# High parts of the first operands written by GpSimd's DMA queue, cast on the way

## The chip, the cores and the metric

One core of one Trainium2 chip runs the whole kernel. The metric is the device time of that core in microseconds. Before the change the median of three runs was 393.45 us (393.07 to 393.51); one further execution was taken with the profiler, and its own time was 392.84 us. All positions in time below count from the start of the profiled span.

## What is computed

Two branches work on the same tokens x (2048 x 448), and a gate mixes them:

```
g   = sigmoid((x * gate_w).sum(-1))                 # one number per token
qkv = x @ wqkv                                      # 448 -> 3 x 448, 16 heads of 28
a   = softmax(q . k over 8 earlier tokens, step 2) . v, then @ wo
b   = relu(x @ w1 + b1)^2 @ w2 + b2                 # 448 -> 1792 -> 448
out = g * a + (1 - g) * b
```

Everything is float32.

## The kernel before

**Splitting.** TensorE multiplies in the type float32r, which keeps fewer bits than float32. So each operand is held as a high part (the float32 value copied into a float32r tile) and a low part (raw value minus high part, again float32r), and each product is made of three matmuls: high times high, high times low, low times high. ACT usually makes the high part by a Copy, DVE the low part by a `tensor_sub`. The raw float32 data must be in SBUF for both.

**Order of the work.** The tokens are cut into four chunks of 512. The inner dimension of 448 is cut in three tiles of 128 (k = 0, 1, 2) and a rest of 64 (written `x7`, `x8` for the tokens' high and low part, `w7h`, `w7l` for the weights). Chunk 0's q projection is the first real work (`qkv_first`, lines 415 to 443): for each k it does, for tokens 0-1 and then 2-3 of the four token tiles (for k > 0 all four at once), `x.h` times `wqh`, `x.h` times `wql`, `x.l` times `wqh`. That is 12 matmuls for each k, 36 in all, all issued at line 429. Each has 452 columns. After them come the rest of 64 rows and then all other projections, as pairs of half-height matmuls from line 341. The order of TensorE's instructions is the order of the program.

**The start.** Line 806 issues `WARM` = 19 matmuls on zeros (256 columns each), which have nothing to wait for. Beside them the first data come in. ACT's queue brings the first k tile of chunk 0's tokens in two halves (`rx[:, 0]`, line 813; 128 partitions x 256 numbers, 128 KB each). SP's queue brings, one after the other, the first weights for k = 0 (`raws[0][:, 0]`, line 816, 225 KB), weights k = 1, tokens k = 1 (line 821, 256 KB), weights k = 2, tokens k = 2, the weights' rest in two pieces (line 819), the tokens' rest, and then six tiles of further weights (line 825) and one more (line 828). GpSimd's queue brings nothing.

Lines 830 to 843 then make high and low parts in this order: for k = 0 `wqh` on ACT (line 831), the first 256 tokens' `x.h` as a cast on DVE (line 836), `wql` on DVE (line 838), their `x.l` on DVE (line 839); then the second 256 tokens' `x.h` on ACT (line 834) and `x.l` on DVE. For k = 1 and 2: `wqh` and `x.h` on ACT, `wql` and `x.l` on DVE. Last come `w7h`, `w7l`, `x7`, `x8`.

**The planner.** All later work of ACT, DVE, POOL and SP is put in order by a planner (`Plan`) that walks along TensorE's order with a clock of its own, `plan.t`. Line 846 sets that clock to `START` = 4900 ns for the first real matmul, and `FIRST` gives the lengths of the first three passes. Lines 847 to 849 give the other engines' first free times as constants.

**GpSimd** clears the attention mask (lines 239 to 241: one memset of the whole, seven of one partition) and `halo0`, the zeros that stand before the first token (line 306). The attention that reads the mask starts after chunk 1; `halo0` is stored by a DMA planned at 24 us.

**The tile `b1z`** holds the bias b1 in its columns 0 to 13 and a zero in column 15 (`none`, written by DVE at line 804).

Of the kernel before, what the change touches and what calls it, by code (L numbers as in the profile page):

```python
# [9 lines left out]
AF = mybir.ActivationFunctionType  # L10
# [6 lines left out]
HALO = W - 1  # L17
# [6 lines left out]
NQ = D + 2  # L24
# [7 lines left out]
MM448, MM512 = 189.2, 216.0  # L32
PE_LAT = 175.0
LAT = 60.0
START = 4900.0
ORDER = (3, 0, 1, 2)
WARM = 19
FIRST = (2700.0, 2350.0, 2300.0)
PP_BUFS = 4
ST_BUFS = 3  # L40
# [143 lines left out]
def gated_mix_kernel(ctx: ExitStack, tc: tile.TileContext, xT, wqkv, w1, w2, wo, b1, b2, out):  # L184
    nc = tc.nc

    def f32(ap):
        return ap.bitcast(F32)
# [35 lines left out]
    mask = const.tile([P, NS, W], F32, name="mask")  # L224
# [11 lines left out]
    b1z = biasp.tile([P, 16], F32, name="b1z")  # L236
    b1t, none = b1z[:, :NF], b1z[0:1, 15:16]
    ctx.enter_context(tc.manual_schedule())
    nc.gpsimd.memset(mask, 0.0)
    for s in range(HALO):  # L240
        nc.gpsimd.memset(mask[0:1, s, 0:HALO - s], -1e9)

# [35 lines left out]
    def x_slot(j, o=16):  # L280
        return x_place[0][:, o + 2 * CH * j:o + 2 * CH * (j + 1)].rearrange("p (i n) -> p i n", i=2)

    def x_tiles(c):
        if c % 2:
            x_place[0] = xpool.tile([P, 8 * CH + 16], F32R, tag="x", name=f"x{c}")
            return [x_slot(j, 0 if c == 1 else 16) for j in range(4)]
        return [xap.tile([P, 2, CH], F32R, tag=f"x{j}", name=f"x{c}_{j}") for j in range(4)]
# [11 lines left out]
    wqh = ap.tile([P, 3, NP + 2 * D], F32R, name="wqh")  # L299
    wql = ap.tile([P, 3, NP + 2 * D], F32R, name="wql")  # L300
# [2 lines left out]
    ap.tile([P, 48], F32, name="pad_a")  # L303

    halo0 = smp.tile([2 * G * HALO, C], F32, tag="lg", name="halo0")
    nc.gpsimd.memset(halo0, 0.0)

    stage = {}
    stores = {(d, par): [] for d in range(3) for par in range(2)}
# [495 lines left out]

    for _ in range(WARM):
        nc.tensor.matmul(warm[:, :2 * P].rearrange("p (i n) -> p i n", i=2), zero, zeros, start=True, stop=True)  # L807

    raws = [rawp.tile([P, 4, 512], F32, tag="raw", name="wqraw0")]
    rx = rawp.tile([P, 4, 512], F32, tag="raw", name="xraw0")  # L810
    halves = slice(0, 256), slice(256, CH)
    for cols in halves:
        nc.scalar.dma_start(rx[:, 0, cols], xT[0, :, 0, cols])
    for k in range(4):
        if k < 3:
            nc.sync.dma_start(raws[0][:, k, :NQ], wqkv[0, :, k])
# [9 lines left out]
        raws.append(raw)  # L826
    raw7 = attp.tile([P, D], F32, tag="q", name="wqraw7")
    nc.sync.dma_start(raw7, wqkv[2, :, 3, :D])
    x = X(x_tiles(0))
    for k in range(3):  # L830
        nc.scalar.activation(wqh[:, k, :NQ], raws[0][:, k, :NQ], AF.Copy)
        for n, cols in enumerate(halves if k == 0 else (slice(0, CH),)):
            if k or n:
                nc.scalar.activation(x.h[k][:, cols], rx[:, k, cols], AF.Copy)
            else:
                nc.vector.tensor_copy(x.h[k][:, cols], rx[:, k, cols])
            if not n:
                nc.vector.tensor_sub(wql[:, k, :NQ], raws[0][:, k, :NQ], f32(wqh[:, k, :NQ]))
            nc.vector.tensor_sub(x.l[k][:, cols], rx[:, k, cols], f32(x.h[k][:, cols]))
    nc.scalar.activation(w7h[:, :NQ], raws[0][:, 3, :NQ], AF.Copy)  # L840
    nc.vector.tensor_sub(w7l[:, :NQ], raws[0][:, 3, :NQ], f32(w7h[:, :NQ]))
# [3 lines left out]

    plan.t, plan.wire = START, 15000.0
    plan.now = 9800.0
# [64 lines left out]
    for c in range(4):  # L912
        x = xs[c]
# [337 lines left out]
    for g in range(2, 2 * NF):  # L1251
# [5 lines left out]
        if not f:  # L1257
            x, slots = X([nxt[j][0] for j in range(4)]), [nxt[j][1] for j in range(4)]
# [105 lines left out]
```

## Time and profile before

| what | value |
|---|---|
| median of three runs | 393.45 us |
| the profiled execution, its own time | 392.84 us |
| its span in the trace | 391.1 us |
| TensorE busy | 386.5 us, 99% of the span |
| DVE, ACT, POOL busy | 260.3, 205.4, 260.6 us |
| data moved by DMA | 73.75 MB, all from SP's queue but for 0.38 MB |

A row of the timeline has the start in us, the length in us, the engine, the line, the operation and its tiles, how many instructions are merged in it (x2), and in brackets how long the engine had been idle and who ended that. Matmuls overlap: one of 452 columns is shown with 0.35 us, but the next one starts 0.19 us after it, so rates are read from starts. PEld is the load of the stationary operand. A row of the table of stages has the stretch, the busy time of each engine with its instructions, the granted TensorE clock, the mean busy share of the 16 DMA engines, and what they moved in GB/s (1 GB/s over 1 us is 1 KB). In the table of DMA issues the last column is the median time from issue to landing.

### The profile page before, as it was taken

How to read it: one execution, taken by the hardware profiler on the slowest of the kernel's cores; microseconds unless marked ns; L12 is line 12 of the kernel's file. 1: busy time of each engine (PE TensorE's matmuls, PEld its weight loads, DVE VectorE, ACT ScalarE, POOL GpSimd, SP SyncE). 2: the span in 40 equal slices, each digit the busy share in tenths (PEclk: the TensorE clock that was granted, in tenths of full speed). 3: DMA queues.
4: the chain of work that ended last, by engine and by line, in shares of the span. 5: the costliest groups of instructions: out<-in, count | busy, mean ns of one | idle time of the engine just before them, and what ended most of it. 6: DMA issues, size and time to landing. Idle time of an engine off the chain costs nothing.

```text
span 391.1 us, 9273 instructions
## 1 busy us (share of the span) xinstructions
PE 386.5 (99%) x3829; PEld 385.3 (99%) x3829; DVE 260.3 (67%) x346; ACT 205.4 (53%) x501; POOL 260.6 (67%) x165
## 2 busy tenths in 40 slices
PE   9999999999999999999999999999999999999996
PEld 8999999999999999999999999999999999999995
DVE  4525523588585778778656989789666686668454
ACT  5857865362566566445555445345716343456740
POOL 0000003979999989959999887999998979661000
PEclk9999999999999999999999999999999999999999
DMA  7999999997174062644203779645635220226835
GB/s 240 399 356 318 373 369 355 377 340 267 49 253 151 1 219 80 220 167 164 90 2 137 244 209 271 218 112 141 217 106 166 84 96 2 88 64 164 141 106 189
DMA packets 64697, 73.75 MB, mean 189 GB/s; under 512 B 32336, under 2 KB 57488, under 8 KB 64272
## 3 DMA queue, kind: packets, MB, share of 16 engines
q1 hardware_dynamic: 64224, 72.79, 56.4%
q8 instruction: 30, 0.49, 0.5%
q10 hardware_dynamic: 432, 0.38, 0.3%
q14 instruction: 11, 0.09, 0.1%
HBM read 45.71 MB, written 28.25 MB: 189 GB/s over the span
## 4 chain that ended last, share of the span: by engine, by line
PE 99%; DVE 0%; DVEq 0%; issue 0%
PE b L341 33%; PE h L341 32%; PE qkv L341 23%; PE a L341 7%; PE qkv L429 2%; PE warm L807 1%; PE a L1154 1%; DVE bt_b L1037 0%; DVEq L1359 0%
## 5 line engine op out<-in xcount | busy, mean ns | idle before, releaser
L539 POOL TENSOR_TENSOR pp<-q,k 128x896 f32<-128x896 f32 x56 | 116.8, 2119 | 75.1 <-DMA k<-k_d 63.5
L341 PE MATMUL h<-x,w1h 64*128 64x512 f32 x672 | 122.0, 376 | 0.0
L551 POOL TENSOR_TENSOR pp<-lg,v 128x896 f32<-128x896 f32 x64 | 113.9, 1868 | 9.4 <-DVE o L561 5.0
L341 PE MATMUL qkv<-wqh,x 64*128 64x448 f32 (+1 forms) x528 | 83.2, 350 | 0.0
L341 PEld LDWEIGHTS h<-x,w1h 64*128 64x128 f32 x672 | 82.8, 186 | 0.0
L341 PE MATMUL h<-x,w1l 64*128 64x512 f32 x336 | 75.9, 376 | 0.0
L793 DVE TENSOR_TENSOR h<-h,h 128x512 fp32r<-128x512 f32 x56 | 38.7, 691 | 55.1 <-ACT h L792 54.9
L543 DVE TENSOR_REDUCE lg<-pp 128x32 f32<-128x896 f32 x64 | 66.9, 1076 | 12.5 <-POOL pp L539 12.5
L341 PE MATMUL b<-w2bh,h 64*128 64x448 f32 x448 | 69.5, 349 | 0.0
L341 PE MATMUL b<-w2ah,h 64*128 64x448 f32 x448 | 69.2, 349 | 0.0
L561 DVE TENSOR_REDUCE o<-pp 128x112 f32<-128x896 f32 x64 | 67.5, 1066 | 0.0
L341 PEld LDWEIGHTS qkv<-wqh,x 64*128 64x128 f32 x528 | 61.0, 186 | 0.0
L341 PE MATMUL qkv<-wql,x 64*128 64x448 f32 (+1 forms) x264 | 56.8, 350 | 0.0
L789 ACT ACTIVATE h<-h,b1z 128x512 f32<-128x512 f32 x56 | 36.7, 655 | 37.1 <-PE h L341 37.1
L341 PEld LDWEIGHTS b<-w2bh,h 64*128 64x128 f32 x448 | 53.2, 193 | 0.0
L341 PEld LDWEIGHTS b<-w2ah,h 64*128 64x128 f32 x448 | 53.1, 193 | 0.0
L341 PE MATMUL b<-w2bl,h 64*128 64x448 f32 x224 | 47.6, 349 | 0.0
L341 PE MATMUL b<-w2al,h 64*128 64x448 f32 x224 | 47.5, 349 | 0.0
L341 PEld LDWEIGHTS h<-x,w1l 64*128 64x128 f32 x336 | 44.0, 186 | 0.0
L791 ACT ACTIVATE h<-h 128x512 fp32r<-128x512 f32 x56 | 33.4, 597 | 1.6
L363 ACT ACTIVATE st<-qkv 128x448 f32<-128x448 f32 x48 | 24.3, 539 | 17.8 <-PE qkv L341 11.5
L341 PEld LDWEIGHTS qkv<-wql,x 64*128 64x128 f32 x264 | 33.2, 186 | 0.0
(108 smaller groups left out, 576.4 us busy)
## 6 DMA issues: line engine op xcount, KB each, us to landing
v<-v_d SPq DMA_DIRECT2D x8, 840.0 KB, 6.8
x_d<-x SPq DMA_DIRECT2D x12, 512.0 KB, 7.3
x<-x_d SPq DMA_DIRECT2D x12, 512.0 KB, 4.1
k<-k_d SPq DMA_DIRECT2D x7, 840.0 KB, 7.4
q_d<-st SPq DMA_DIRECT2D x8, 448.0 KB, 5.8
k_d<-st SPq DMA_DIRECT2D x8, 448.0 KB, 5.7
v_d<-st SPq DMA_DIRECT2D x8, 448.0 KB, 6.4
o_d<-o SPq DMA_DIRECT2D x16, 224.0 KB, 2.1
```

The costliest lines, as they stand in the source:

```text
L341: nc.tensor.matmul(woven_out(acc.pt, acc.n), a[rows], woven(w[rows]), start=acc.todo == acc.all, stop=acc.todo == 1)
L363: nc.scalar.activation(st[0][:, :, t % 2].rearrange("p (i g) c -> p i g c", i=2), unwoven(pt[:, :D]).rearrange("p i (g c) -> p i g c", c=C ...
L429: nc.tensor.matmul(woven_out(acc.pt, NQ), a, woven(w), start=k == j == 0, stop=False)
L539: nc.gpsimd.tensor_mul(pr.rearrange("p (w c) -> p w c", w=W), q[:, s:s + 1].to_broadcast([P, W, C]), k[:, s:s + W])
L543: nc.vector.tensor_reduce(lgs[i][:, s], pr.rearrange("p (w h d) -> p w h d", w=W, h=HG), axis=AX.X, op=ALU.add)
L551: nc.gpsimd.tensor_mul(pr.rearrange("p (h d w) -> p w h d", h=HG, w=W), lgs[i][:, s][:, :, :, None].to_broadcast([P, W, HG, DH]), vs[i][:, ...
L561: nc.vector.tensor_reduce(o_t[par, s][:, g * C:(g + 1) * C], pr.rearrange("p (c w) -> p c w", w=W), axis=AX.X, op=ALU.add)
L789: a = add(ACT, 656.0, lambda pt=pt, r=r: nc.scalar.activation(pt, pt, AF.Relu, bias=b1t[:, f + r:f + r + 1]), ready, bias_job[0], prio=NEXT)
L791: b = add(ACT, 600.0, lambda pt=pt, hh=hh: nc.scalar.activation(hh, pt, AF.Square), a, prio=NEXT)
L793: low = add(DVE, 690.0, lambda pt=pt, hh=hh, hl=hl: nc.vector.tensor_sub(hl, pt, f32(hh)), a, prio=NEXT)
L807: nc.tensor.matmul(warm[:, :2 * P].rearrange("p (i n) -> p i n", i=2), zero, zeros, start=True, stop=True)
L1154: nc.tensor.matmul(woven_out(acc.pt, D), a, woven(w), start=False, stop=acc.todo == 1)
```

## The change

The high parts of the k = 0 weights (`wqh[:, 0]`, 128 x 450) and of the first 256 tokens (`x.h[0][:, :256]`) are written straight from DRAM by two DMAs on GpSimd's queue, whose destination is float32r while the source is float32. ACT's Copy and DVE's cast that made them go away. The raw data are still brought, since the low parts need them: the weights by SP's queue as before, the tokens' first k tile by ACT's queue, now in one DMA of 512 columns in place of two of 256. GpSimd's memsets are issued behind its two DMAs. A Copy of one number into an unused column of `b1z` is put on ACT ahead of its other work. `WARM` goes from 19 to 17 and `START` from 4900 to 4650.

```diff
-START = 4900.0
+START = 4650.0
...
-WARM = 19
+WARM = 17
...
-    nc.gpsimd.memset(mask, 0.0)
-    for s in range(HALO):
-        nc.gpsimd.memset(mask[0:1, s, 0:HALO - s], -1e9)
...
-    nc.gpsimd.memset(halo0, 0.0)
...
+    x = X(x_tiles(0))
+    nc.gpsimd.dma_start(wqh[:, 0, :NQ], wqkv[0, :, 0])
+    nc.gpsimd.dma_start(x.h[0][:, :256], xT[0, :, 0, :256])
+    nc.gpsimd.memset(mask, 0.0)
+    for s in range(HALO):
+        nc.gpsimd.memset(mask[0:1, s, 0:HALO - s], -1e9)
+    nc.gpsimd.memset(halo0, 0.0)
     raws = [rawp.tile([P, 4, 512], F32, tag="raw", name="wqraw0")]
     rx = rawp.tile([P, 4, 512], F32, tag="raw", name="xraw0")
     halves = slice(0, 256), slice(256, CH)
-    for cols in halves:
-        nc.scalar.dma_start(rx[:, 0, cols], xT[0, :, 0, cols])
+    nc.scalar.dma_start(rx[:, 0], xT[0, :, 0])
+    nc.scalar.activation(b1z[0:1, 14:15], none, AF.Copy)
...
-    x = X(x_tiles(0))
     for k in range(3):
-        nc.scalar.activation(wqh[:, k, :NQ], raws[0][:, k, :NQ], AF.Copy)
+        if k:
+            nc.scalar.activation(wqh[:, k, :NQ], raws[0][:, k, :NQ], AF.Copy)
+        nc.vector.tensor_sub(wql[:, k, :NQ], raws[0][:, k, :NQ], f32(wqh[:, k, :NQ]))
         for n, cols in enumerate(halves if k == 0 else (slice(0, CH),)):
             if k or n:
                 nc.scalar.activation(x.h[k][:, cols], rx[:, k, cols], AF.Copy)
-            else:
-                nc.vector.tensor_copy(x.h[k][:, cols], rx[:, k, cols])
-            if not n:
-                nc.vector.tensor_sub(wql[:, k, :NQ], raws[0][:, k, :NQ], f32(wqh[:, k, :NQ]))
             nc.vector.tensor_sub(x.l[k][:, cols], rx[:, k, cols], f32(x.h[k][:, cols]))
```

## The prediction

> **What bounds the kernel now.** I read the page first, then the chain of work that ended last, then the timeline of the first 12 us, then the stages of 1 us. The page:
>
> ```profile
> span 391.1 us, 9273 instructions
> PE 386.5 (99%) x3829; PEld 385.3 (99%) x3829; DVE 260.3 (67%) x346; ACT 205.4 (53%) x501; POOL 260.6 (67%) x165
> ```
>
> TensorE is busy from end to end. The chain says the same: it is TensorE alone, zeros first, then the 36 matmuls of line 429, then the long stream of line 341.
>
> ```profile
> 0.79 4.39 PE warm L807 x19
> 5.18 7.10 PE qkv L429 x36
> 12.28 86.71 PE qkv L341 x911
> ```
>
> Behind 12.28 there is next to nothing to win, and the change takes away no matmul of use. It can only move the moment at which the dense stream begins. So the question is when the first matmuls start and whether the operands keep up with them. These rows carry the answer:
>
> ```profile
> 4.22 0.58 ACT L831 ACTIVATE wqh<-wqraw 128x450 fp32r<-128x450 f32 x1 [1.27 <-DMA wqraw<-wqkv]
> 4.40 0.29 DVE L836 CAST x<-xraw 128x256 fp32r<-128x256 f32 x1 [3.54 <-DMA xraw<-xT]
> 4.84 0.63 DVE L838 TENSOR_TENSOR wql<-wqraw,wqh 128x450 fp32r<-128x450 f32 x1
> 4.97 0.69 PE L429 MATMUL qkv<-wqh,x 128*128 128x452 f32 x2
> 5.38 0.42 DVE L839 TENSOR_TENSOR x<-xraw,x 128x256 fp32r<-128x256 f32 x1
> 5.52 0.65 PE L429 MATMUL qkv<-wql,x 128*128 128x452 f32 x2
> 5.55 0.42 ACT L834 ACTIVATE x<-xraw 128x256 fp32r<-128x256 f32 x1 [0.75 <-DMA xraw<-xT]
> 5.88 0.56 ACT L831 ACTIVATE wqh<-wqraw 128x450 fp32r<-128x450 f32 x1
> 6.34 0.61 ACT L834 ACTIVATE x<-xraw 128x512 fp32r<-128x512 f32 x1
> 7.15 1.31 PE L429 MATMUL qkv<-wqh,x 128*128 128x452 f32 x6
> 8.08 0.63 ACT L834 ACTIVATE x<-xraw 128x512 fp32r<-128x512 f32 x1 [0.65 <-DMA xraw<-xT]
> 9.06 1.69 PE L429 MATMUL qkv<-wqh,x 128*128 128x452 f32 x8
> 9.79 0.63 ACT L842 ACTIVATE x<-xraw 128x512 fp32r<-128x512 f32 x1 [0.38 <-DMA xraw<-xT]
> 10.46 0.69 DVE L843 TENSOR_TENSOR x<-xraw,x 128x512 fp32r<-128x512 f32 x1 [0.38 <-ACT x L842]
> 10.59 0.93 PE L429 MATMUL qkv<-wql,x 128*128 128x452 f32 x4
> ```
>
> The weights land at 4.22 and are copied by 4.80; the first tokens land at 4.40 and are cast by 4.69. The first real matmul starts at 4.97, just where the zeros end: 19 take (4.97 - 0.79) / 19 = 0.220 us each, 0.86 ns a column. In the dense part eight matmuls go from 9.06 to 10.59, 0.191 us each for 452 columns, 0.42 ns a column: the array runs at half its rate under the zeros. The first two real ones still take 5.52 - 4.97 = 0.55 us together, so the rate doubles at about 5.2.
>
> A mark for later: matmul 13, the first of k = 1, is the third of the six of the row at 7.15, so it starts at 7.15 + 2 x 0.191 = 7.53. It needs the k = 1 tokens' high part, ready at 6.34 + 0.61 = 6.95: 0.58 to spare. Matmul 25 (k = 2) starts at 7.53 + 12 x 0.191 = 9.82 and its tokens are ready at 8.71, 1.1 to spare. The rest is due near 12.2; `x7` is ready at 10.42, `x8` at 11.15 and needed two pairs later, so over 1.4 to spare.
>
> **The change part by part.**
>
> *Removed before the first matmul.* ACT's 0.58 and DVE's 0.29, and 2 x 0.220 = 0.44 of zeros, which now end at 0.79 + 17 x 0.220 = 4.53. Real matmuls cannot start before that. Starting 0.44 earlier would not be worth 0.44: until about 5.2 each would take 452 x 0.86 = 0.39 us in place of 0.19, so the gain is about half, 0.2, with up to 0.15 more from waits that might vanish (the first 12 matmuls take 7.53 - 4.97 = 2.56, against 12 x 0.191 = 2.29).
>
> *Added: 361 KB of DMA.* The two new DMAs read 128 x 450 x 4 = 230 KB and 128 x 256 x 4 = 131 KB, and no raw transfer goes away. The stages show what the engines have free:
>
> ```profile
> 1.00:2.00 1.00, 1.00 (x6) 1.00 (x7) 0.00 (x0) 0.33 (x1) 0.39 (x8) 1.00 0.26 43
> 2.00:3.00 1.00, 1.00 (x6) 1.00 (x6) 0.00 (x0) 0.95 (x1) 0.00 (x0) 1.00 0.66 189
> 3.00:4.00 1.00, 1.00 (x7) 1.00 (x6) 0.00 (x0) 0.00 (x0) 0.00 (x0) 1.00 0.93 280
> 4.00:5.00 1.00, 1.00 (x7) 1.00 (x6) 0.46 (x2) 0.58 (x1) 0.00 (x0) 1.00 0.94 299
> 5.00:6.00 1.00, 1.00 (x5) 0.75 (x5) 0.80 (x2) 0.45 (x2) 0.00 (x0) 1.00 1.02 376
> 6.00:7.00 1.00, 1.00 (x7) 0.99 (x7) 0.95 (x2) 1.00 (x3) 0.00 (x0) 1.00 1.00 381
> ```
>
> From 3 us on the 16 engines are full. At 380 GB/s the 361 KB are 0.95 us of all of them; from 2 to 5 us they idle 0.34 + 0.07 + 0.06 = 0.47 us, which a third queue may fill. So whatever lands last of the k = 1 data comes 0.5 to 0.95 later. Up to the k = 1 tokens the queues carry 230 + 262 + 230 + 262 = 984 KB; the stages' sum (43, 232, 512, 811, 1187, 1568 KB at 2 to 7 us) passes that at 5.46. Landings come after the bytes: the first 361 KB are through at 3.46 and land at 4.22 and 4.40, 0.76 to 0.94 later. So these tokens land near 6.3 now, and at 6.8 to 7.25 afterwards; with ACT's 0.61 and 0.1 to the matmul, 13 can start at 7.5 to 7.95. I take 7.7, the middle: **0.2 later** than 7.53.
>
> *The landing of POOL's two DMAs,* call it L. No transfer of POOL's queue is in this trace, so I bound it:
>
> ```profile
> bt_b<-f_d SPq DMA_DIRECT2D x12, 224.0 KB, 3.1
> xraw<-xT ACTq DMA_DIRECT2D x2, 128.0 KB, 4.3
> wqraw<-wqkv SPq DMA_DIRECT2D x3, 225.0 KB, 4.1
> w2raw<-w SPq DMA_DIRECT2D x1, 896.0 KB, 9.2
> ```
>
> POOL's first rows in the timeline:
>
> ```profile
> 0.74 0.15 POOL L239 MEMSET mask<- 128x64 f32 x1 [0.29 <-POOLq L1356]
> 0.95 0.31 POOL L241 MEMSET mask<- 1x7 f32 x7
> 1.21 0.18 POOL L306 MEMSET halo<- 56x112 f32 x1
> ```
>
> POOL is free to issue at 0.74. The low end is 3.1 us, a transfer of this size with less beside it: L = 3.85. The far end is 9.2: L = 9.95. The nearest rows are the same tensors, at the same time, beside another queue: 4.1 and 4.3. I take 4.25, **L = 5.0**. With 0.13 to the start, as from 4.84 (high parts done at 4.80) to 4.97, the first matmul starts at 5.13, after the zeros, and at the full rate from about 5.2. Matmul 13 could then start at 5.13 + 2.29 + about 0.1 = 7.5, inside the 7.7 that the k = 1 tokens allow.
>
> *The low parts of k = 0.* The raw weights land at 4.22 now; if POOL's 230 KB share the wire with them they come 0.6 later, 4.8, so `wql` (0.63) is ready at 5.63 behind L = 5.0 and matmul 3 is due at 5.13 + 0.1 + 0.38 = 5.6. The first `x.l` follows at 6.05, matmul 5 is due at 6.0. The second `x.h` needs the whole token tile, whose second half lands at 5.55 now: it has ACT to itself, is ready at 6.0 to 6.5, and matmul 7 is due at 6.4. All within 0.1.
>
> *Cost nothing:* POOL's 0.64 us of memsets move behind two DMA issues (the first reader is a DMA planned at 24 us); ACT's one issue less (0.43) and its one-number Copy, since ACT is idle for 1.27 us before 4.22; SP's order, unless an issue must wait for POOL's landing, and the data that SP issues after 3 us stand behind 2 us of queue. The k = 2 tokens and the rest come up to 0.95 later with 1.1 and 1.4 to spare. `START` moves the planner's clock by 0.25 us against constants of 10 us and more; ACT and DVE have a third to a half of their time free, so nothing to under 0.3 either way.
>
> **Sum:** +0.2 us. On the profiled execution's span 391.1 -> 391.3, its own time 392.84 -> 393.04. The median of the runs stands 0.61 above that execution, so **393.65 us**. A measurement of this kernel tells about 0.2%, 0.79 us, from no change.
>
> **The rivals.**
>
> *The gain as meant.* POOL's bytes land by 4.5, using the time in which the engines are a quarter and two thirds busy. Matmul 1 starts at 4.53, and 13 at 7.2 to 7.4: 393.1 to 393.3. Against it: the k = 1 tokens, at 7.5 or more by my sum. The Trainium skill, "DMA: Bandwidth & Descriptors", section "Anatomy of one DMA — SWDGE (gpsimd) path", fits such a transfer by 2.0 us plus its bytes at 436 GB/s; by that estimate, 2.83 us for both, they would land near 3.6 and this rival would hold. No run here shows it yet, and the two rows of SP's and ACT's queues, 4.1 and 4.3 us, are slower than that fit. A gain over 0.79 is all but out: even with the zeros' end at 4.53 and the full rate at once, 13 starts at 6.82, 0.71 earlier.
>
> *POOL's queue served last* (slower). SP's 128 rows of 1800 B and ACT's of 1024 B landed together, 4.22 and 4.40, as if the engines took rows from the queues in turn. POOL's 256 rows would then end with SP's first 256 (460 KB) and ACT's 128 of 2 KB (262 KB): 1083 KB, through at 5.72, less up to 0.47, and landed 0.8 later, L = 6.05 to 6.5. Then 13 starts at L + 0.13 + 2.29 = 8.5 to 8.9: +0.95 to +1.4, 394.4 to 394.85. It decides from L = 5.9 (5.9 + 2.42 = 7.53 + 0.79). Against it: the engines' free 0.47, and POOL issues no later than the others.
>
> *A long first latency on POOL's queue.* Each us of L beyond 5.9 adds 1 us: L = 7.2 to 9.95 gives 395.7 to 398.4. Nothing in the trace speaks for it, and nothing excludes it.
>
> *The rate doubles later.* The doubling came after 5.2 - 0.79 = 4.4 us of unbroken matmuls. If two zeros less and a pause from 4.53 to 5.13 make it start anew, it comes near 9.5, and the time from 5.2 to 9.5 counts half: +2.1, 395.8. The Trainium skill, "TensorE: Matmul & The Clock Gate", "Part 1: The HAM clock gate", says that the gate opens after a busy window that does not begin with the kernel; a pause of 0.6 us may or may not spoil one. No row here can tell.
>
> *The change doesn't do what it says* (the cast on the way leaves other bits): the same bytes and instructions, so no other time.
>
> **How the numbers follow.** Forecast (393.3 to 394.2) 0.54; gain as meant 0.08; gain over 0.79 by all of it together 0.02; POOL served last 0.20; long latency 0.12; late doubling 0.04. The first two lie within 0.2%: 0.62. The last three are slower: 0.36. Faster: 0.02. The range runs from 393.0, below the gain as meant, to 395.0, above POOL served last; it leaves out the long latency, the late doubling and the small gain, under 2 in 10.
>
> **What would show it.** Right: the first matmul of line 429 at 4.9 to 5.4, its wait ended by a DMA of POOL's queue; matmul 13 at 7.5 to 7.95, behind ACT's Copy of the k = 1 tokens that starts at 6.85 to 7.25; DMA share near 1 from 2.5 us; the rows behind 12.3 as now, all moved by the same amount. Wrong: a first matmul at 4.5 (the gain), or after 6 (served last, or latency; POOL's landing time tells which, by whether raw data land before it), 0.39 us steps after 5.5 (the rate), or idle time on TensorE behind 13 us, for which I have no term.

## The result, and the profile after

The change made the kernel slower: 398.59 us median (397.92 to 399.13, four runs) against 393.31 us (393.07 to 393.51, four runs), a ratio of 1.0133, 95% interval 1.012 to 1.0147. The forecast was 393.65 in a range up to 395.0. The profiled execution after is the longest of its four, 399.13 us with a span of 397.4; against the profiled one of before that is 6.3 us of span, more than the 5.3 us between the medians. The accounts below are of those two executions.

The page and the chain of work of the kernel after; the chain's columns are start, length, what:

```profile
span 397.4 us, 9272 instructions
PE 388.4 (98%) x3827; PEld 386.7 (97%) x3827; DVE 261.7 (66%) x345; ACT 205.6 (52%) x501; POOL 261.6 (66%) x167
```

```profile
1.25 0.72 POOL wqh L806
1.97 6.93 DMA x<-xT
8.90 0.14 issue
9.03 9.44 PE qkv L425 x36
```

Where the chain was TensorE from 0.79 us on, it now begins with POOL: two DMA issues at 1.25 and 1.97, and 6.93 us from the second issue to its landing at 8.90. Only then do the 36 matmuls begin, at 9.03 in place of 4.97. The timeline of the kernel after shows what they then do:

```profile
5.68 0.42 ACT L838 ACTIVATE x<-xraw 128x256 fp32r<-128x256 f32 x1 [3.00 <-DMA xraw<-xT]
7.43 0.63 DVE L835 TENSOR_TENSOR wql<-wqraw,wqh 128x450 fp32r<-128x450 f32 x1 [6.56 <-DMA wqh<-wqkv]
7.67 0.63 ACT L838 ACTIVATE x<-xraw 128x512 fp32r<-128x512 f32 x1 [0.79 <-DMA xraw<-xT]
9.03 1.09 PE L425 MATMUL qkv<-wqh,x 128*128 128x452 f32 x2 [4.28 <-DMA x<-xT]
10.67 1.71 PE L425 MATMUL qkv<-wqh,x 128*128 128x452 f32 x4
12.18 0.96 PE L425 MATMUL qkv<-wql,x 128*128 128x452 f32 x2
15.26 1.69 PE L425 MATMUL qkv<-wqh,x 128*128 128x452 f32 x8
16.78 0.93 PE L425 MATMUL qkv<-wql,x 128*128 128x452 f32 x4
18.40 0.46 PE L337 MATMUL qkv<-w7h,x 64*128 64x452 f32 x2
```

Four matmuls from 10.67 to 12.18 are 0.378 us each: half the rate. Eight from 15.26 to 16.78 are 0.190 each: the full rate. The step between starts changes near 13.8, and the trace's record of the granted clock begins there, with 1.00. (Ahead of its first record the clock column in the tables of stages stands at 1.00 whatever the rate, so there the rate is read from starts.) So there are two losses. The first matmul is 9.03 - 4.97 = 4.06 us later. The 36 matmuls take 18.40 - 9.03 = 9.37 us, where before they took 12.21 - 4.97 = 7.24: 2.13 more. Together 6.19, and the span grew by 6.3: behind the 36 all is as dense as before.

The table of DMA issues of the kernel after, with the median time from issue to landing in the last column:

```profile
wqraw<-wqkv SPq DMA_DIRECT2D x3, 225.0 KB, 5.1
xraw<-xT ACTq DMA_DIRECT2D x1, 256.0 KB, 4.9
wqh<-wqkv POOLq DMA_DIRECT2D x1, 225.0 KB, 6.2
x<-xT POOLq DMA_DIRECT2D x1, 128.0 KB, 6.9
```

POOL's two transfers take 6.2 and 6.9 us. SP's are slower than before too: 5.1 against 4.1 for the weights.

### The profile page after: what moved, and what is told of

The parts are those of the page before. It is cut to its first block, busy times and chain, and to the rows that moved or that the text cites. A ratio compares the mean times of both kernels' runs of the same rounds, so it can differ in the third digit from the quotient of the medians.

```text
span 397.4 us, 9272 instructions
## 1 busy us (share of the span) xinstructions
PE 388.4 (98%) x3827; PEld 386.7 (97%) x3827; DVE 261.7 (66%) x345; ACT 205.6 (52%) x501; POOL 261.6 (66%) x167
## 4 chain that ended last, share of the span: by engine, by line
PE 97%; DMA 2%; issue 0%; POOL 0%; DVE 0%; DVEq 0%; POOLq 0%
PE b L337 32%; PE h L337 32%; PE qkv L337 22%; PE a L337 7%; PE qkv L425 2%; DMA x<-xT 2%; PE a L1154 1%; POOL wqh L806 0%; DVE bt_b L1037 0%; DVEq L1359 0%; POOLq L1356 0%
```

## The experiments

The theory at this point: POOL's queue starts late by itself, sharing the engines adds to it, and the pause of TensorE from 4.5 to 9.0 costs half the rate afterwards. The rivals: the cast is slow; the sharing alone is to blame; the slow matmuls wait for late operands.

**Zeros to bridge the pause** (the kernel after):

```diff
-WARM = 17
+WARM = 55
```

> The kernel after, with 55 matmuls on zeros in place of 17, so that TensorE has work until POOL's data land near 8.9 us. My theory: the 6.3 us of the profiled execution are 4.06 us of later first matmul (9.03 against 4.97) and 2.1 us of half rate from 9.0 to 13.8, because the pause from 4.5 to 9.0 undid what the zeros had done. Then the rate doubles near 5.2 under the zeros and stays, the first real matmul comes at 9.0 to 9.2, all 36 matmuls step by 0.191 us, the span is 395.0 to 395.3, the median near 396.5. Rival: the slow steps come from low parts or tokens that arrive late, then they stay at 0.375 us or wait, and the time stays at 398.6.

Measured: 397.01 us median (396.74 to 397.49), ratio to before 1.0094 (1.0076 to 1.0111); the profiled span 395.5. Its timeline:

```profile
8.31 1.39 PE L803 MATMUL warm<-const-float32-0.0 128*128 128x256 f32 x11
9.03 0.76 DVE L839 TENSOR_TENSOR x<-xraw,x 128x256 fp32r<-128x256 f32 x2 [0.88 <-DMA x<-xT]
9.54 0.55 PE L425 MATMUL qkv<-wqh,x 128*128 128x452 f32 x2
13.36 1.69 PE L425 MATMUL qkv<-wqh,x 128*128 128x452 f32 x8
14.89 0.93 PE L425 MATMUL qkv<-wql,x 128*128 128x452 f32 x4
16.51 0.46 PE L337 MATMUL qkv<-w7h,x 64*128 64x452 f32 x2
```

POOL's data land at 9.0 as before the edit, but the 36 matmuls now take 16.51 - 9.54 = 6.97 us, 2.40 less than in the kernel after, about 0.191 apart. The operands came within 0.1 us of the same times, so they were not what held the matmuls to 0.378: the half rate came from TensorE's having stood idle until then. The time is 0.5 above the forecast because the zeros were too many. In this execution the rate doubled only near 6.1, not 5.2, so 55 zeros ended at 9.54 and not at 9.0.

**The same DMAs with nobody waiting** (the kernel before, into an unused place):

```diff
+    spare = early[:, 0, 0:2].rearrange("p a d -> p (a d)").bitcast(F32R)
+    nc.gpsimd.dma_start(spare[:, :NQ], wqkv[0, :, 0])
+    nc.gpsimd.dma_start(spare[:, 512:768], xT[0, :, 0, :256])
     raws = [rawp.tile([P, 4, 512], F32, tag="raw", name="wqraw0")]
```

> The kernel before, with the same two DMAs on POOL's queue written to an unused place, so that nobody waits for them: the sharing of the DMA engines alone. My theory: the wait for POOL's landing is what costs; beside it the raw data come up to 0.95 us later, so the first real matmul is at 5.0 to 5.9 and the time 393.3 to 394.5. Rival: the added bytes themselves hold everything up, then it is over 396.

Measured: 393.72 us median against 393.2, ratio 1.0007 (0.9998 to 1.0017): not told from no change. Its timeline and its DMA issues:

```profile
5.03 0.98 PE L429 MATMUL qkv<-wqh,x 128*128 128x452 f32 x2
6.40 0.42 ACT L837 ACTIVATE x<-xraw 128x256 fp32r<-128x256 f32 x1 [1.42 <-DMA xraw<-xT]
7.74 1.31 PE L429 MATMUL qkv<-wqh,x 128*128 128x452 f32 x6
9.94 0.63 ACT L837 ACTIVATE x<-xraw 128x512 fp32r<-128x512 f32 x1 [0.61 <-DMA xraw<-xT]
```

```profile
early<-wqkv POOLq DMA_DIRECT2D x1, 225.0 KB, 6.5
early<-xT POOLq DMA_DIRECT2D x1, 128.0 KB, 7.4
```

The first matmul is at 5.03, nearly as before; the second token half lands at 6.40 in place of 5.55; matmul 13 starts at 7.74 + 0.38 = 8.12 in place of 7.53. POOL's transfers are as late as in the kernel after, 6.5 and 7.4, but here nothing waits for them. So the added bytes cost at most 0.7 us (the interval's end); the wait for POOL's landing, with the half rate behind it, costs the rest.

**No cast** (the kernel before; POOL brings raw data, ACT and DVE make the high parts):

```diff
-    for cols in halves:
-        nc.scalar.dma_start(rx[:, 0, cols], xT[0, :, 0, cols])
-    for k in range(4):
+    nc.gpsimd.dma_start(raws[0][:, 0, :NQ], wqkv[0, :, 0])
+    nc.gpsimd.dma_start(rx[:, 0, halves[0]], xT[0, :, 0, halves[0]])
+    nc.scalar.dma_start(rx[:, 0, halves[1]], xT[0, :, 0, halves[1]])
+    for k in range(1, 4):
```

> The kernel before, with the raw first weights and the raw first 256 tokens brought by POOL's queue without a cast, and the high parts made by ACT and DVE as before: no byte more than before. My theory, POOL's queue itself starts late: its first bytes at about 4.4 us, landing at 6 to 7.5, the first real matmul at 6.8 to 8.2. Rival, the cast on the way is slow: then without it the queue lands at 4.2 to 4.5 as SP's and ACT's do, and the time is that of before.

Measured: 399.78 us (one run). Its DMA issues:

```profile
wqraw<-wqkv POOLq DMA_DIRECT2D x1, 225.0 KB, 6.2
xraw<-xT POOLq DMA_DIRECT2D x1, 128.0 KB, 6.9
```

6.2 and 6.9, to the tenth as with the cast. The transfers are as late without a cast, so the cast is not the cause, and neither are added bytes, for there are none here. The landings, 7.7 and 9.1, are later than I had written (6 to 7.5); the first matmul came at 9.57.

**The same transfers on ACT's queue** (the kernel before):

```diff
-    for cols in halves:
+    nc.scalar.dma_start(raws[0][:, 0, :NQ], wqkv[0, :, 0])
+    for cols in halves:
         nc.scalar.dma_start(rx[:, 0, cols], xT[0, :, 0, cols])
-    for k in range(4):
+    for k in range(1, 4):
```

> The kernel before, with the raw first weights put on ACT's queue ahead of the tokens' two halves, SP's queue beginning with the k = 1 weights: the same transfers as in e3_nocast, but on ACT's queue in place of POOL's. My theory now: it is POOL's queue that gets little of the DMA engines while others are busy (alone it landed 3.3 us after its first issue, beside them 7.6), so on ACT's queue the same 361 KB land at 4.2 to 5.2, and the time is within 1 us of before. Rival: any third of the data that shares with a busy SP queue is that late, then they land at 7 to 9 and the time is over 397.

Measured: 396.69 us median, ratio 1.0091 (1.0074 to 1.0108). Its timeline:

```profile
4.39 0.58 ACT L832 ACTIVATE wqh<-wqraw 128x450 fp32r<-128x450 f32 x1 [0.96 <-DMA wqraw<-wqkv]
6.38 0.29 DVE L837 CAST x<-xraw 128x256 fp32r<-128x256 f32 x1 [5.52 <-DMA xraw<-xT]
6.82 1.09 PE L429 MATMUL qkv<-wqh,x 128*128 128x452 f32 x2 [1.65 <-DVE x L837]
```

Neither theory holds whole. The weights land at 4.4, 3.3 us before they do on POOL's queue; the tokens behind them at 6.4, 2.7 before POOL's 9.1, yet 2.0 later than before. So a transfer that stands second on ACT's queue beside SP's full one is late too, and POOL's two land 2.7 to 3.3 us later still. Of that, 0.8 and 1.0 us are POOL's later issue: 1.51 and 2.21 against 0.74 and 1.18. The time of this run also holds half rate: the matmuls from 7.71 to 8.46 step by 0.375 us, and the rate doubles only at 9.8.

**POOL alone** (the kernel before; POOL's two DMAs go into the raw data's place, so the other queues wait for them):

```diff
+    nc.gpsimd.dma_start(raws[0][:, 0, :NQ].bitcast(F32R), wqkv[0, :, 0])
+    nc.gpsimd.dma_start(rx[:, 0, halves[0]].bitcast(F32R), xT[0, :, 0, halves[0]])
     for cols in halves:
         nc.scalar.dma_start(rx[:, 0, cols], xT[0, :, 0, cols])
```

> The kernel before, with POOL's two casting DMAs first, into the place of the raw data, so that SP's and ACT's first loads of the same place wait for them: POOL's queue with the DMA engines to itself. (Its total time says nothing, since all the raw data come later.) My theory: the first bytes come 3.1 us after the issue at 1.25 even so, at 4.4, and the 361 KB take about 1 us more, landing at 6.1 to 6.5; so 2.4 to 2.8 of the 8.9 are the sharing. Rival, POOL was late only because the other queues were served first: then bytes start at 2.2 to 2.6 and land by 4.2.

Measured (399.57 us in all, one run). Its DMA issues:

```profile
wqraw<-wqkv POOLq DMA_DIRECT2D x1, 225.0 KB, 3.0
xraw<-xT POOLq DMA_DIRECT2D x1, 128.0 KB, 2.6
```

With idle engines POOL's transfers take 3.0 and 2.6 us, nearer to the rival (landed by 4.2) than to my 6.1 to 6.5. The issue is at 1.49, the first bytes at 2.89, the landings at 4.5 and 4.8. My theory that the late first bytes are POOL's own (3.1 us after the issue in the kernel after) falls: alone they come 1.4 us after it. What delays them in the kernel is the other queues' traffic.

**Half the traffic beside it** (the kernel after):

```diff
     for k in range(4):
+        if k == 1:
+            nc.vector.tensor_copy(raws[0][0:1, 1, 0:1], f32(wqh)[0:1, 0, 0:1])
```

> The kernel after, with SP's loads from k = 1 on held until POOL's first weights have landed (DVE copies one of their numbers into the place of the next load); beside POOL's 361 KB there are only 492 KB of raw data. My theory, sharing: POOL's weights land at 5.0 to 5.8 in place of 7.40 and the tokens soon behind, 5.5 to 6.5 in place of 8.90; the k = 1 data then are what matmul 13 waits for, at 8.5 to 9.5. Rival, a fixed delay of POOL's queue whenever another queue runs at all: landings at 7 or later.

Measured (398.15 us in all, one run). Its DMA issues, then two rows of its timeline:

```profile
wqh<-wqkv POOLq DMA_DIRECT2D x1, 225.0 KB, 4.8
x<-xT POOLq DMA_DIRECT2D x1, 128.0 KB, 4.4
```

```profile
6.54 0.62 PE L425 MATMUL qkv<-wqh,x 128*128 128x452 f32 x2 [1.81 <-DMA x<-xT]
10.95 1.46 PE L425 MATMUL qkv<-wqh,x 128*128 128x452 f32 x4 [1.87 <-ACT x L840]
```

4.8 and 4.4, between alone and full. The tokens' landing at 6.4 is in the range that sharing gave, the weights' at 6.0 is 0.2 above it. The time stays within the spread of the kernel after (397.92 to 399.13): matmul 13 now waits until 10.95 for the held k = 1 data, 1.4 us beyond what I had written, and behind this second pause, 1.87 us, the half rate is back: the four matmuls from 12.20 to 13.71 step by 0.378.

**POOL first** (the kernel after; two one-number memsets by POOL in the places of the raw data, ahead of the mask's, hold SP's and ACT's first loads):

```diff
+    nc.gpsimd.memset(raws[0][0:1, 0, 0:1], 0.0)
+    nc.gpsimd.memset(rx[0:1, 0, 0:1], 0.0)
     nc.gpsimd.memset(mask, 0.0)
```

> The kernel after, with SP's and ACT's first loads held until POOL has issued its two DMAs (two memsets of one number by POOL in the places of the raw data), at about 2.6 us in place of 0.75. My theory: POOL's rows are late because the engines are full when they come; with the engines empty its first bytes come at 2.6 to 2.9, 1.4 after the issue as it was alone, and both land by 5.0 to 5.5, with the raw data at 6 to 7. Rival, the share alone counts and not who comes first: then POOL's last lands at 7 or later.

Measured (399.6 us in all, one run). Its DMA issues, then its timeline:

```profile
wqh<-wqkv POOLq DMA_DIRECT2D x1, 225.0 KB, 3.1
x<-xT POOLq DMA_DIRECT2D x1, 128.0 KB, 2.8
```

```profile
2.61 0.86 SPq L821 DMA_DIRECT2D wqraw<-wqkv  x2
4.92 0.62 PE L425 MATMUL qkv<-wqh,x 128*128 128x452 f32 x2 [0.17 <-DMA x<-xT]
8.66 0.63 DVE L837 TENSOR_TENSOR wql<-wqraw,wqh 128x450 fp32r<-128x450 f32 x1 [7.79 <-DMA wqraw<-wqkv]
9.34 1.12 PE L425 MATMUL qkv<-wql,x 128*128 128x452 f32 x2 [3.80 <-DVE wql L837]
```

With 1.4 us of a head start POOL's data land at 4.3 and 4.8, and the first real matmul starts at 4.92, the earliest of all kernels here that start with POOL's data. But the raw weights, issued at 2.61, land only near 8.6: 6 us, where I had expected 6 to 7 as the landing time. `wql` is then late, and the third matmul starts at 9.34. Nothing is won by going first: here the raw data come second and are late, and the first three matmuls need the high parts and the low parts.

**The same pair once more, later** (the kernel of the second experiment, and behind the last line of the first low parts):

```diff
+    nc.vector.tensor_copy(spare[:, 447:448], x.x8[:, 0:1])
+    nc.vector.tensor_copy(spare[:, 767:768], x.x8[:, 0:1])
+    nc.gpsimd.dma_start(spare[:, :NQ], wqkv[0, :, 0])
+    nc.gpsimd.dma_start(spare[:, 512:768], xT[0, :, 0, :256])
```

> The kernel before, with the two POOL DMAs to an unused place as in e2_beside, and the same two once more behind the last of the first low parts, near 11.5 us, when SP's queue keeps the engines full. My theory: the second pair is as late as the first, 2.5 us or more from issue to first bytes and 6 or more to the last landing. Rival, a cost of the queue's first use: then the second pair's first bytes come 1.0 to 1.5 us after the issue.

Measured (394.57 us, one run). Rows of its timeline and its DMA issues, the latter with the median over both pairs:

```profile
1.48 0.72 POOL L810 DMA_DIRECT2D early<-wqkv  x1
7.37 1.31 PE L429 MATMUL qkv<-wqh,x 128*128 128x452 f32 x6
12.75 0.53 POOL L849 DMA_DIRECT2D early<-wqkv  x1 [10.01 <-DVE early L848]
```

```profile
early<-wqkv POOLq DMA_DIRECT2D x2, 225.0 KB, 7.5
early<-xT POOLq DMA_DIRECT2D x2, 128.0 KB, 8.1
```

The second pair is not faster but slower: landings at 21.4 and 22.4, 8.7 and 9.1 us after the issues, with first bytes at 16.5, 3.7 us after. A cost of first use is out. The 16 engines were fuller around the second pair: a share of 1.02 to 1.13 in every stage from 13 to 21 us, against 0.55 to 0.92 from 2 to 5 us around the first.

## Why the prediction was wrong

**What bounds the kernel:** right. Only the start of the dense stream moved, and what stands behind 12.2 us kept its length: 6.19 us of shift at the first matmul of line 337, 6.3 at the end.

**The landing of POOL's DMAs, L = 5.0:** this step failed. I bounded L by 3.85 and 9.95 and took the nearest rows, 4.1 and 4.3 us for the same tensors on SP's and ACT's queues. Measured were 6.2 and 6.9, L = 8.90. The rows were near in size and in time but not in what decides: SP's and ACT's transfers were issued from 0.74 on, ahead of POOL's, while POOL's come behind them, to engines busy 0.65 of the time from 2 to 3 us and 0.88 from 3 to 4. The first of POOL's bytes came 3.1 us after the issue there, 1.4 with empty engines. The issue itself came at 1.25 and 1.97, not at 0.74 for both.

**The rival "POOL's queue served last"** named the right cause (the landings depend on the traffic beside: 3.0, 4.8, 6.2, 8.7 us for the weights from none to full), but its price was too small: it put the landing at 6.05 to 6.5. Its mechanism, rows taken in turn, does not explain 8.90, since the first bytes are late as well. The rival "a long first latency" had the right size (L between 7.2 and 9.95) and, taken as POOL's own delay, the wrong reason: alone, the first bytes come 1.4 us after the issue. (Its times were summed a little high: 393.45 + 2.09 and + 4.84 are 395.54 and 398.29, not 395.7 and 398.4.)

**The 2.0 us plus bytes of the Trainium skill,** "DMA: Bandwidth & Descriptors", section "Anatomy of one DMA — SWDGE (gpsimd) path", give 2.5 and 2.3 us for the two. Alone, the runs here show 3.0 and 2.6, the order of it; in the kernel, 6.2 and 6.9. So here the fit comes near with idle engines alone. The Trainium skill's other rule on that page, section "Issuing engines are not separate DMA queues", that all queues run on the same 16 engines and interleave, is what these runs bear out: where POOL's data came earlier, the raw data came later.

**The late doubling of the rate,** to which I gave 0.04, happened: 2.13 us. I had tied it to a short pause, 4.53 to 5.13; the pause was 4.5 us long, and the 17 zeros had ended before the rate doubled at all (the last two still start 0.213 us apart). The chance should have hung on L: a late L makes the half rate likely, so the two rivals add up rather than exclude each other. That is how 8.90, which by the first latency's own line (L + 2.42 against 7.53) gives +3.8, became +6.2: the bridging zeros took 2.40 of it away. The Trainium skill, "TensorE: Matmul & The Clock Gate", "Part 1: The HAM clock gate", has the array fall back to half rate after an idle window of about 3.4 us and double again after a busy one. The traces agree in part: the kernel after doubles 4.7 us after its restart, and in the run without a cast, where the rate had doubled and TensorE then stood idle for 5.0 us, the granted clock falls to 0.50 (the first row below). With half the traffic, though, a pause of 1.87 us was enough for it (the second row), and one of 1.81 us, before 6.54, was not: what decides between these two is not settled here.

```profile
8.00:9.00 1.00, 0.00 (x0) 0.00 (x0) 0.00 (x0) 1.00 (x4) 0.00 (x0) 0.50 1.09 269
12.00:13.00 1.00, 1.00 (x5) 0.88 (x4) 0.43 (x1) 0.55 (x1) 0.00 (x0) 0.50 1.04 231
```

**The sharing of the wire:** right in kind, too small for the landing. I put the k = 1 tokens' Copy at 6.85 to 7.25 and it started at 7.67. I had priced the 361 KB at 380 GB/s, but from 3 to 5 us the stages that I read show 280 and 299 GB/s at a share of 0.93 and 0.94, which makes 1.2 to 1.3 us of them instead of 0.95. What it costs matmul 13 is not fixed: with nobody waiting for POOL it came 0.59 later, where I had taken 0.2; in the run with the pair once more, which starts alike, it came at 7.37 + 0.38 = 7.75, 0.22 later.

**Costs at nothing:** they hold, one of them by luck. The k = 2 tokens, put at up to 0.95 later with 1.1 to spare, came 2.1 later (Copy at 10.18 against 8.08); nothing waited for them only because the matmuls were later still. With nobody waiting for POOL, their Copy ends at 9.94 + 0.63 = 10.57 and matmul 25 starts behind it, at 10.62 instead of 10.41. The moved memsets, ACT's Copy and the planner's start left no row on the chain, and TensorE has no new idle time behind 13 us.

I found no version that beats the kernel before. The head start shows why: the low parts need the raw data too, and with the operand brought twice one of the two came late each time.

## What to carry to other kernels

In these runs a transfer's time went by its place in the traffic more than by its size: before putting a critical load on another queue, look at what the other queues have issued ahead of it, and price it by a transfer that came second, not by the one that came first. Where the first matmul may come late, ask also whether TensorE then pauses long enough to run at half rate; here the two costs came together. Bringing data a second time to save a conversion of 0.6 us paid in none of the runs here.

## What the runs showed of the hardware

- A cast from float32 to float32r on the way accounts for little of the delay: 6.2 and 6.9 us with it and without it (without it, 361 KB less were moved beside), and 3.0 and 2.6 with it when nothing else moved.
- POOL's transfer of 225 KB landed 3.0 us after its issue with idle engines, 4.8 beside 492 KB of other loads, 6.2 beside SP's full sequence, 8.7 in the middle of it; the same 225 KB at the head of ACT's queue, issued at 0.74 beside SP's first one, landed at 4.4.
- The delay goes both ways: SP's 225 KB, issued as POOL's rows began to move, took 6 us, although the engines were not full. The stages of that run, with the DMA share and GB/s at the end:

```profile
4.00:5.00 1.00, 0.83 (x5) 0.57 (x4) 0.00 (x0) 0.55 (x2) 0.00 (x0) 1.00 0.77 77
5.00:6.00 1.00, 0.54 (x2) 0.19 (x2) 0.00 (x0) 0.00 (x0) 0.00 (x0) 1.00 0.53 148
```

  What holds the second comer while engines are idle stays open; no run here looks inside a queue.
- Where the zeros lasted long enough, the trace has the rate of TensorE double at 3.7 us (no cast), 4.4 (POOL alone), 5.2 (before) and 6.1 (55 zeros); in the run on ACT's queue, with the 19 zeros of before, they ended too early and it doubles at 9.8. So a fixed count of zeros does not fit every execution. Whether this makes the spread of 1.2 us among the four runs after was not tried.
